# Top-k attention and an ELU layer: one chunk transposed later, weight differences one a step, two stores together

## The chip, the cores and the metric

The kernel runs on one core of a Trainium2 chip. A core has engines that run side by side, each through its own list of instructions in order: TensorE (PE; its weight loads are shown as PEld), VectorE (DVE), ScalarE (ACT), GpSimd (POOL) and SyncE (SP), which here only issues DMAs. They meet through semaphores. PE writes to PSUM, a small memory in banks of 512 float32 per partition; the other data lies in SBUF, 128 partitions wide. The metric is the device time of one execution in microseconds (us), the median of several runs.

## The reference

All is float32, apart from the layer's weights, which arrive as float64 and are taken apart by the kernel at the start.

```python
batch, n_heads, seq, head_dim = 8, 8, 576, 64
scores = q @ k.T / sqrt(64)                       # per head, 576 x 576
kth    = 32nd largest of each row
scores = where(scores >= kth, scores, -1e9)
attn   = softmax(scores)
x      = (attn @ v), heads joined                 # 4608 x 512
h      = x @ w_in                                 # 512 x 2048
g      = where(h > 0, h, exp(min(h, 0)) - 1)
out    = g @ w_out                                # 2048 x 512, out 4608 x 512
```

## The kernel before, in words

**Steps.** The attention is cut into 144 steps, 18 per batch element. A step is one tile of 128 queries for a pair of heads (in the last two steps of an element, or the first two, 64 queries of four heads). The main loop over `n` (L805) interleaves four stages of different tiles: scores of step n+2 on PE (`scores`, L326), the selection of the 32 largest of step n on DVE (`select`, L348: four MAX8 and three MATCH_REPLACE8 per head), the masked exponential of step n-1 on ACT and POOL (`spread` L373, `mask` L380, `normalise` L401), and of step n-2 the transposition of the probabilities on PE (`turn`, L418) with the product by v (`attend`, L443) when a group of tiles is complete.

**Turning.** The probabilities of a step are 2 x 576 columns, nine chunks of 128. `main` is chunks 0 to 3, `rest` is chunk 4 (the last keys of the first head and the first of the second), `other` is chunks 5 to 8. `main` and `other` go through PSUM tiles of a pool of two (`ps_t`), `rest` through columns 288 to 415 of a bank that also holds half of the scores of one head (`wide[1][:, 1, ...]`, columns 0 to 287). ACT copies each to SBUF (`et`, L434).

**The layer.** x is collected into blocks, 5 of one tile of 128 tokens at the start, 15 of two tiles, and one of one tile at the end. A block is a list of pieces: 16 `hidden` pieces (x @ w_in, ELU on ACT, POOL and DVE), and for a block of two tiles 7 `product` pieces (j = 0 to 6, and a last j = 7 that only empties a list), in which the product with w_out is made from seven products of half-size quarters, with sums on POOL (`combine`, L579). Four of the seven use differences of quarters of w_out (t1 to t4). These are made once on POOL, stored in DRAM (`kept`, L686) and streamed back for every block in tiles `tw` of two chunks from a pool of six (`stream`, L658; L666); a product consumes four such tiles and asks for a new one after each. `emit` (L582) stores one tile of a block's result.

**Order.** PE, ACT, DVE and POOL run in the order in which the program issues their instructions. SP is not in that list (L780): the order of its DMAs is set by the scheduler, which knows dependencies and its own estimates of time, and SP then works through that order without overtaking. `feed` (L763) is called four times a step, after each of DVE's four passes, and issues pieces of the layer when a running account says that they are due, so that the work is spread over the steps; what is left at the end follows in a row (L840). `at` (L741) puts loads and other calls at the start of a chosen step. In `load_halves` q and k of a head pair go into a pool of two buffers each (`kin`, `qin`), which DVE transposes into one of five `kqT` buffers (L289).

The step's own part of the loop, around the change:

```python
        if done:
            turn(done, main)
            turn(done, rest)
        if prev:
            mask(prev, 1, n <= tight)
        next(passes)
        feed(n, 0.25)
        if done:
            turn(done, other)
        next(passes)
        if prev:
            normalise(prev)
        feed(n, 0.25)
```

Of the kernel before, what the change touches and what calls it, by code (L numbers as in the profile page):

```python
# [9 lines left out]
ALU = mybir.AluOpType  # L10
FP32 = mybir.dt.float32
# [69 lines left out]
def kernel(  # L81
# [9 lines left out]
    nc = tc.nc  # L91
    P = nc.NUM_PARTITIONS
    B, H, S, D = q.shape
    dm, dff = moe_w_in.shape[0], moe_w_in.shape[1] // 2
# [9 lines left out]
    W = dm // 2  # L104
    TF, TB = 2, 6
    QT = NG // TF
# [294 lines left out]
    def normalise(u):  # L401

        if u.normal:
            return
        u.normal = True
        den = small.tile([P, 2], FP32, tag="dene", name="dene")
        nc.gpsimd.tensor_scalar_add(den[:], u.den[:, 0:2], EPS)  # L407
        rec = small.tile([P, 2], FP32, tag="rec", name="rec")
        nc.gpsimd.tensor_tensor(rec[:], den[:], power[:], ALU.pow)
        nc.gpsimd.tensor_tensor(den[:], den[:], rec[:], ALU.mult)  # L410
        nc.gpsimd.tensor_scalar(den[:], den[:], -1.0, 2.0, ALU.mult, ALU.add)
        nc.gpsimd.tensor_tensor(rec[:], rec[:], den[:], ALU.mult)
        for i in range(2):
            nc.gpsimd.tensor_scalar(  # L414
                u.sc[:, i, :], u.sc[:, i, :], rec[:, i : i + 1], 1.0, ALU.mult, ALU.mult
            )

    def turn(u, chunks):  # L418

        if u.turned:  # L420
            return
        g = u.group
        if g.et is None:
            g.et = etpool.tile([P, 2 * J + 1, len(g.tiles), P], FP32, tag="et", name="et")
        if chunks.stop - chunks.start == 1:
            ps = wide[1][:, 1, HS : HS + P]
        else:
            ps = ps_t.tile([P, JP], FP32, tag="t", name="eps")
        sc = u.sc[:, :, :].rearrange("p i s -> p (i s)")
        n = chunks.stop - chunks.start  # L430
        for c in range(n):
            c0 = (chunks.start + c) * P
            nc.tensor.transpose(ps[:, c * P : (c + 1) * P], sc[:, c0 : c0 + P], ident[:])  # L433
        nc.scalar.copy(  # L434
            g.et[:, chunks, u.at, :],
            ps[:, 0 : n * P].rearrange("p (c q) -> p c q", c=n),
        )
        if chunks.stop == 2 * J + 1:
            u.turned = True
            if u.at == len(g.tiles) - 1:  # L440
                closing.append(g)
# [68 lines left out]
    def ffn_pieces(blk):  # L510
# [71 lines left out]
        def emit(s):  # L582
            for t in blk.tiles[s]:
                p0 = t.cols.start - s * P
                nc.sync.dma_start(out[t.rows, :], blk.o[s][p0 : p0 + t.ql, :])

        def product(j):
            left, right = slice(0, W), slice(W, dm)
            while blk.after:
                blk.after.pop(0)()  # L590
            if j == 7:
                return
            if j == 0:
                close_gates(upto=(blk.number, NF - 1))
                blk.o = [opool.tile([P, dm], FP32, tag="osb", name="osb") for _ in range(2)]
                blk.e = [late["e"].tile([P, W], FP32, tag="e", name="e") for _ in range(2)]
                blk.s = [ps_f.tile([P, dm], FP32, tag="f", name="ops") for _ in range(2)]
            a11, a12 = quarter(0, 0), quarter(0, 1)
            a21, a22 = quarter(1, 0), quarter(1, 1)
            c11, c12 = blk.o[0][:, left], blk.o[0][:, right]  # L600
            c21, c22 = blk.o[1][:, left], blk.o[1][:, right]
            e0, e1 = blk.e[0][:], blk.e[1][:]
            one, two, three = blk.s[0][:, left], blk.s[1][:, left], blk.s[1][:, right]
            x, name, sums, opens, dst, after = (
                (a11, "b11", one, True, c11, [(a21, a21, a22, ALU.add)]),
                (a12, "b21", two, True, e0, [(a11, a21, a11, ALU.subtract)]),
                (a21, "t1", three, True, c22, [
                    (a12, a12, a11, ALU.subtract), (c11, c11, e0, ALU.add),
                ]),
                (a11, "t2", one, False, c12, [(a21, a22, a11, ALU.subtract)]),  # L610
                (a12, "b22", three, False, e1, [(c12, c12, e1, ALU.add)]),
                (a21, "t3", one, False, c21, [(c22, c22, c21, ALU.add)]),
                (a22, "t4", two, True, e0, [(c21, c21, e0, ALU.add)]),
            )[j]
            if j == 0:
                combine(*after.pop(0))
            for f in range(NG):
                if name[0] == "b":
                    w = w_out[:, NG * (name[1] == "2") + f, right if name[2] == "2" else left]
                else:  # L620
                    if f % TF == 0:
                        t = streamed.pop(0)
                    w = t[:, f % TF, :]
                nc.tensor.matmul(  # L624
                    sums, x[:, f, :], w, start=opens and f == 0, stop=f == NG - 1,
                    skip_group_check=not opens,
                )
                if name[0] == "t" and f % TF == TF - 1:
                    stream()
            if 0 < j < 4:  # L630
                combine(*after.pop(0))
            nc.scalar.copy(dst, sums)
            blk.after += [lambda x=x: combine(*x) for x in after]
            if j in (4, 6):
                blk.after.append(lambda: emit(j // 2 - 2))

        part = HIDDEN[blk.slots]
        behind = 2 * NF if blk.number else 0
# [27 lines left out]
        nc.sync.dma_start(t[:], src[:].rearrange("p (f n) -> p f n", f=TF))  # L666
        streamed.append(t)

    kept = {}

    def differences(q):

        fs = slice(q * TF, (q + 1) * TF)
        low = slice(NG + q * TF, NG + (q + 1) * TF)
        b11, b12 = w_out[:, fs, 0:W], w_out[:, fs, W:dm]
        b21, b22 = w_out[:, low, 0:W], w_out[:, low, W:dm]
        made = {}
        for name, x, y in (
            ("t1", b12, b11), ("t2", b22, "t1"), ("t4", b21, "t2"), ("t3", b22, b12),
        ):  # L680
            t = late["t"].tile([P, TF, W], FP32, tag="t", name="tw")
            made[name] = t
            y = made[y][:] if isinstance(y, str) else y
            nc.gpsimd.tensor_tensor(t[:], x, y, ALU.subtract)  # L684
            kept[name, q] = scratch.tile([P, TF * W], FP32, tag=f"{name}{q}", name="kept")
            nc.sync.dma_start(  # L686
                kept[name, q][:].rearrange("p (f n) -> p f n", f=TF), t[:]
            )

    ffn = []  # L690
    steps, first, due = [], {}, []
# [49 lines left out]
    def at(step, fn, *args):  # L741
        todo.setdefault(step, []).append((fn, args))
# [10 lines left out]
            at(f - ready, start_qk, b, hp)  # L753
            at(f - late_v, load_v, b, hp)

    for x in range(QT):
        at(first[1] - 2 + 2 * x, differences, x)
    for _ in range(TB):
        at(first[1] - 2 + 2 * QT, stream)

    fed = {"at": 0.0, "sum": 0.0, "over": 0.0}

    def feed(n, share):  # L763

        place[0] += 1
        close_gates(2 if n > tight + 3 else 6)
        fed["at"] = max(fed["at"], n)
        ahead = [(w - fed["sum"]) / (x - fed["at"]) for x, w in due if x > fed["at"]]
        if ahead:
            fed["over"] += max(0.0, share * min(ahead))  # L770
        fed["at"] += share
        while ffn and decoded[0] >= ffn[0][1] and 0.5 * ffn[0][0] <= fed["over"]:
            cost, _, piece, _ = ffn.pop(0)
            fed["over"] -= cost
            fed["sum"] += cost
            piece()
            settle()
# [27 lines left out]
    for n in range(NS + 3):  # L805
        for fn, args in todo.pop(n, []):
            fn(*args)
        ahead, cur, prev, done = step(n + 2), step(n), step(n - 1), step(n - 2)
        passes = select(cur, n < tight) if cur else iter(range(4))
        if prev and n > tight:  # L810
            spread(prev)
        next(passes)
        feed(n, 0.25)
        if ahead and n > 1:
            scores(ahead)
        while closing:
            attend(closing.pop(0))
        if prev:
            mask(prev, 0, n <= tight)
        if n > 1:  # L820
            turn_qk()
        next(passes)
        feed(n, 0.25)
        if done:
            turn(done, main)
            turn(done, rest)
        if prev:
            mask(prev, 1, n <= tight)
        next(passes)
        feed(n, 0.25)  # L830
        if done:
            turn(done, other)
        next(passes)
        if prev:
            normalise(prev)
        feed(n, 0.25)
        turn_qk(True)
        if n < 2:
            scores(ahead)
# [36 lines left out]
```

## Time and profile before

| what | us |
|---|---|
| median of 3 runs (lowest, highest) | 1604.12 (1603.91, 1605.75) |
| the profiled execution: its time, its span | 1605.63, 1603.8 |
| PE busy | 1523.6 (95%) |
| DVE busy | 1452.6 (91%) |
| ACT busy | 1200.0 (75%) |
| POOL busy | 903.3 (56%) |
| DMA queue of SP, share of 16 engines | 28.0% |

A line of the groups or of the timeline gives the kernel's line (L433), the engine, the operation, what it writes and reads by the program's names, and behind the bar or in brackets how long the engine was idle just before and what ended that. A line of the waits gives who waited for what, the total in us, how often, and the longest. PEld is PE's loading of weights, SPq is SP's queue of issues. A busy PE is modelled, since matmuls are pipelined; the granted clock is the share of full speed that TensorE had.

### The profile page before, as it was taken

To read this page: it belongs to the slowest core of one execution; us is meant where nothing else is said; L and a number is where in the kernel's file an instruction comes from. 1 tells how busy PE (TensorE), PEld (TensorE's weight loads), DVE (VectorE), ACT (ScalarE), POOL (GpSimd) and SP (SyncE) were. 2 spreads that over 40 slices of the span, in tenths; PEclk is the share of its full clock that TensorE was granted. 3 is DMA by queue.
4 is the path that set the end of the run, shared out by engine and by line. 5 is a ranking of instruction groups with operands and counts; after the bars stand their busy time and mean duration, and the time that the engine had idled before them with its cause. 6 is when DMAs were issued, how large, how long until landed. Compare 5 with 4: busy or idle time off the path is not lost.

```text
span 1603.8 us, 28233 instructions
## 1 busy us (share of the span) xinstructions
PE 1523.6 (95%) x9492; PEld 1182.3 (74%) x9492; DVE 1452.6 (91%) x2976; ACT 1200.0 (75%) x2460; POOL 903.3 (56%) x1551
## 2 busy tenths in 40 slices
PE   4789999999999999999999999998999999999999
PEld 2477667757777778876887788776777777877786
DVE  6999999999999799999999599999999969999700
ACT  6997676778686869695878787876878777878652
POOL 4984455446456465646565656564656565656550
PEclk9889989999999999999999999999999999999999
DMA  8622323012503251403421343114230413030411
GB/s 242 195 80 37 68 66 114 8 22 46 148 1 119 36 141 32 119 16 90 96 81 47 88 91 95 56 53 103 60 112 15 119 38 112 10 118 1 119 53 34
DMA packets 224912, 123.47 MB, mean 77 GB/s; under 512 B 182272, under 2 KB 183296, under 8 KB 224768
## 3 DMA queue, kind: packets, MB, share of 16 engines
q1 hardware_dynamic: 223568, 121.38, 28.0%
q8 instruction: 75, 1.23, 0.3%
q14 instruction: 69, 0.57, 0.1%
q10 hardware_dynamic: 1200, 0.30, 0.1%
HBM read 108.00 MB, written 13.63 MB: 76 GB/s over the span
## 4 chain that ended last, share of the span: by engine, by line
PE 67%; DVE 13%; ACT 11%; POOL 5%; issue 3%; DMA 1%; SPq 0%; DVEq 0%; ACTq 0%; POOLq 0%
PE hps L534 24%; PE ops L624 18%; PE avps L459 8%; PE scps L335 7%; DVE wk L362 6%; PE eps L433 5%; DVE m L369 4%; PE ops L562 2%; ACT sc L397 2%; ACT sc L343 2%; DVE m L355 2%; ACT sc L396 1%; POOL tw L684 1%; ACT et L434 1%; POOL sc L414 1%
## 5 line engine op out<-in xcount | busy, mean ns | idle before, releaser
L369 DVE MAX8 m<-wk 128x8 f32<-128x576 f32 x864 | 609.9, 747 | 3.3 <-POOL den L376 3.2
L534 PE MATMUL hps<-xT,w_in 128*128 128x256 f32 (+1 forms) x2688 | 550.8, 354 | 3.5 <-ACT gT L547 3.5
L534 PEld LDWEIGHTS hps<-xT,w_in 128*128 128x128 f32 x2688 | 442.9, 193 | 63.8 <-issue 15.5
L362 DVE MATCH_REPLACE8 wk<-m,wk 128x576 f32<-128x576 f32 x576 | 423.5, 743 | 0.0
L407 POOL TENSOR_SCALAR dene<-den 128x2 f32<-128x2 f32 x144 | 32.5, 226 | 471.7 <-ACT sc L397 470.4
L397 ACT ACTIVATE sc<-sc,den 128x576 f32<-128x576 f32 x288 | 223.4, 776 | 65.8 <-POOL den L376 51.2
L624 PE MATMUL ops<-tw,gT 128*128 128x256 f32 x960 | 224.5, 387 | 12.8 <-DMA tw<-kept 11.9
L396 ACT ACTIVATE sc<-sc,m 128x576 f32<-128x576 f32 x288 | 225.3, 782 | 11.5 <-DVE m L369 11.5
L343 ACT ACTIVATE sc<-scps 128x576 f32<-128x576 f32 x288 | 170.7, 645 | 73.5 <-PE scps L335 73.4
L414 POOL TENSOR_SCALAR sc<-sc,rec 128x576 f32<-128x576 f32 x288 | 214.4, 756 | 14.9
L335 PE MATMUL scps<-kqT 64*128 64x288 f32 (+1 forms) x1280 | 196.6, 447 | 25.5 <-ACT kqT L311 13.4
L355 DVE MAX8 m<-sc 128x8 f32<-128x576 f32 x288 | 202.2, 744 | 19.1 <-ACT sc L343 18.0
L624 PEld LDWEIGHTS ops<-tw,gT 128*128 128x128 f32 x960 | 178.9, 192 | 46.0 <-DMA tw<-kept 14.5
L362 DVE MATCH_REPLACE8 wk<-m,sc 128x576 f32<-128x576 f32 x288 | 211.7, 743 | 0.0
L459 PE MATMUL avps<-et,vT 128*64 128x256 f32 (+2 forms) x2320 | 197.0, 313 | 9.8 <-ACT et L434 9.8
L459 PEld LDWEIGHTS avps<-et,vT 128*64 128x64 f32 x2320 | 132.9, 142 | 82.2 <-issue 39.9
L504 POOL TENSOR_TENSOR gT<-n,gT 128x512 f32<-128x512 f32 x136 | 173.2, 1279 | 23.9 <-ACT n L553 23.9
L433 PE MATMUL eps<-ident,sc 128*128 128x128 f32 x1152 | 177.3, 279 | 0.5 <-POOL sc L414 0.4
L335 PEld LDWEIGHTS scps<-kqT 64*128 64x128 f32 (+1 forms) x1280 | 104.7, 183 | 94.4 <-issue 40.7
L434 ACT COPY et<-eps 128x512 f32<-128x512 f32 x288 | 164.6, 572 | 10.8 <-PE eps L433 8.4
L433 PEld LDWEIGHTS eps<-ident,sc 128*128 128x128 f32 x1152 | 142.4, 144 | 35.8 <-issue 13.3
L624 PE MATMUL ops<-w_out,gT 128*128 128x256 f32 x720 | 164.3, 381 | 0.1
(56 smaller groups left out, 1540.0 us busy)
## 6 DMA issues: line engine op xcount, KB each, us to landing
tw<-kept SPq DMA_DIRECT2D x240, 256.0 KB, 3.1
raw<-in_moe_w_in_dram SPq DMA_DIRECT2D x16, 512.0 KB, 4.9
vT<-in_v_dram SPq DMA_DIRECT2D x64, 128.0 KB, 2.5
raw<-in_moe_w_out_dram SPq DMA_DIRECT2D x16, 512.0 KB, 4.5
out_dram<-osb SPq DMA_DIRECT2D x32, 256.0 KB, 2.4
kin<-in_k_dram SPq DMA_DIRECT2D x112, 72.0 KB, 2.4
qin<-in_q_dram SPq DMA_DIRECT2D x112, 72.0 KB, 2.6
kept<-tw SPq DMA_DIRECT2D x16, 256.0 KB, 2.0
```

What stands on the lines that cost most here:

```text
L335: nc.tensor.matmul(wide[i][rows, half, 0:HS], kq[part, q0 : q0 + u.t.ql], kq[part, k0 : k0 + HS], start=True, stop=True,)
L343: nc.scalar.activation(u.sc[:, i, :].rearrange("p (a s) -> p a s", a=2), wide[i][:, :, 0:HS], AF.Copy, scale=scale,)
L355: nc.vector.max(found[i], cur[i])
L362: nc.vector.match_replace(wk[i], found[i], cur[i], TAKEN)
L369: nc.vector.max(found[i], cur[i])
L396: nc.scalar.activation(sc, sc, AF.Prelu, scale=-1.0, bias=low, alpha=1.0 / STEEP)
L397: nc.scalar.activation(sc, sc, AF.Exp, scale=-STEEP, bias=gap, accum_out=u.den[:, i : i + 1])
L414: nc.gpsimd.tensor_scalar(u.sc[:, i, :], u.sc[:, i, :], rec[:, i : i + 1], 1.0, ALU.mult, ALU.mult)
L433: nc.tensor.transpose(ps[:, c * P : (c + 1) * P], sc[:, c0 : c0 + P], ident[:])
L459: nc.tensor.matmul(ps[i * D : (i + 1) * D, cols], vt[:, 2 * J + i if c == J else i * J + c, :], w, start=(c == 0), stop=(c == J),)
L534: nc.tensor.matmul(blk.h[:, f % bank, :], w_in[:, i, f * P : (f + 1) * P], blk.xT[:, i, 0:n_tok], start=(i == 0), stop=(i == NC - 1),)
L624: nc.tensor.matmul(sums, x[:, f, :], w, start=opens and f == 0, stop=f == NG - 1, skip_group_check=not opens,)
```

## The change

It has three parts. (1) `turn(done, rest)` moves from directly behind `turn(done, main)` to directly ahead of `turn(done, other)`, so behind `mask(prev, 1)`, DVE's third pass and one call of `feed`. (2) The 16 subtractions that make t1 to t4 (four quarters of each) were issued four at a time at the start of steps 16, 18, 20 and 22; now one is issued in each of steps 16 to 31, behind `normalise` and ahead of the step's last `feed`, and its store with it. The first six streams move from the start of step 24 to the start of step 32. (3) The two stores of a block of two tiles, until now issued behind the sums of product 4 and of product 6, are both issued behind the sums of product 6. SP's order is left to the scheduler before and after.

```diff
             blk.after += [lambda x=x: combine(*x) for x in after]
-            if j in (4, 6):
-                blk.after.append(lambda: emit(j // 2 - 2))
+            if j == 6:
+                blk.after += [lambda s=s: emit(s) for s in range(2)]
...
-    def differences(q):
+    def difference(q, name, x, y):
         fs = slice(q * TF, (q + 1) * TF)
         low = slice(NG + q * TF, NG + (q + 1) * TF)
-        b11, b12 = w_out[:, fs, 0:W], w_out[:, fs, W:dm]
-        b21, b22 = w_out[:, low, 0:W], w_out[:, low, W:dm]
-        made = {}
-        for name, x, y in (
-            ("t1", b12, b11), ("t2", b22, "t1"), ("t4", b21, "t2"), ("t3", b22, b12),
-        ):
-            t = late["t"].tile([P, TF, W], FP32, tag="t", name="tw")
-            made[name] = t
-            y = made[y][:] if isinstance(y, str) else y
-            nc.gpsimd.tensor_tensor(t[:], x, y, ALU.subtract)
-            kept[name, q] = scratch.tile([P, TF * W], FP32, tag=f"{name}{q}", name="kept")
-            nc.sync.dma_start(
-                kept[name, q][:].rearrange("p (f n) -> p f n", f=TF), t[:]
-            )
+        ends = {
+            "b11": w_out[:, fs, 0:W], "b12": w_out[:, fs, W:dm],
+            "b21": w_out[:, low, 0:W], "b22": w_out[:, low, W:dm],
+        }
+        t = late["t"].tile([P, TF, W], FP32, tag="t", name="tw")
+        x, y = (ends[z] if z in ends else made[z, q] for z in (x, y))
+        nc.gpsimd.tensor_tensor(t[:], x, y, ALU.subtract)
+        made[name, q] = t[:]
+        kept[name, q] = scratch.tile([P, TF * W], FP32, tag=f"{name}{q}", name="kept")
+        nc.sync.dma_start(kept[name, q][:].rearrange("p (f n) -> p f n", f=TF), t[:])
...
-    for x in range(QT):
-        at(first[1] - 2 + 2 * x, differences, x)
+    spare = [(q, *names) for q in range(QT) for names in (
+        ("t1", "b12", "b11"), ("t2", "b22", "t1"), ("t4", "b21", "t2"), ("t3", "b22", "b12"))]
     for _ in range(TB):
-        at(first[1] - 2 + 2 * QT, stream)
+        at(first[1] - 2 + len(spare), stream)
...
         if done:
             turn(done, main)
-            turn(done, rest)
         if prev:
             mask(prev, 1, n <= tight)
         next(passes)
         feed(n, 0.25)
         if done:
+            turn(done, rest)
             turn(done, other)
         next(passes)
         if prev:
             normalise(prev)
+        if spare and n >= first[1] - 2:
+            difference(*spare.pop(0))
         feed(n, 0.25)
```

More of the change, by code (lines that the diff above doesn't have):

```diff
@@ L667, in stream @@
         streamed.append(t)
-    kept = {}
-    def differences(q):
+    kept, made = {}, {}
+    def difference(q, name, x, y):
         fs = slice(q * TF, (q + 1) * TF)
         low = slice(NG + q * TF, NG + (q + 1) * TF)
-        b11, b12 = w_out[:, fs, 0:W], w_out[:, fs, W:dm]
-        b21, b22 = w_out[:, low, 0:W], w_out[:, low, W:dm]
-        made = {}
-        for name, x, y in (
-            ("t1", b12, b11), ("t2", b22, "t1"), ("t4", b21, "t2"), ("t3", b22, b12),
-        ):
-            t = late["t"].tile([P, TF, W], FP32, tag="t", name="tw")
-            made[name] = t
-            y = made[y][:] if isinstance(y, str) else y
-            nc.gpsimd.tensor_tensor(t[:], x, y, ALU.subtract)
-            kept[name, q] = scratch.tile([P, TF * W], FP32, tag=f"{name}{q}", name="kept")
-            nc.sync.dma_start(
-                kept[name, q][:].rearrange("p (f n) -> p f n", f=TF), t[:]
-            )
+        ends = {
[8 more added lines that the diff above has]
+        nc.sync.dma_start(kept[name, q][:].rearrange("p (f n) -> p f n", f=TF), t[:])
     ffn = []
@@ L754 @@
             at(f - late_v, load_v, b, hp)
-    for x in range(QT):
-        at(first[1] - 2 + 2 * x, differences, x)
+    spare = [
+        (q, *names)
+        for q in range(QT)
+        for names in (
+            ("t1", "b12", "b11"), ("t2", "b22", "t1"), ("t4", "b21", "t2"),
+            ("t3", "b22", "b12"),
+        )
+    ]
     for _ in range(TB):
-        at(first[1] - 2 + 2 * QT, stream)
+        at(first[1] - 2 + len(spare), stream)
     fed = {"at": 0.0, "sum": 0.0, "over": 0.0}
```

## The prediction

> **What bounds the kernel now.** I read the chain first, then the windows, each engine's waits, and the timelines around the waits that the change touches. The chain of work that ended last, by engine:
>
> ```profile
> PE 67%; DVE 13%; ACT 11%; POOL 5%; issue 3%; DMA 1%; SPq 0%; DVEq 0%; ACTq 0%; POOLq 0%
> ```
>
> Busy times by window (length, then PE, PEld, DVE, ACT, POOL, granted clock):
>
> ```profile
> 286.00:546.00 260.00, 252.94 (x1454) 191.10 (x1452) 249.03 (x512) 203.91 (x416) 136.80 (x253) 1.00 0.22 55
> 560.00:921.00 361.00, 353.75 (x2251) 282.16 (x2255) 344.84 (x709) 276.94 (x572) 212.51 (x364) 1.00 0.30 79
> 1512.00:1603.80 91.80, 88.07 (x505) 71.33 (x504) 3.23 (x5) 40.54 (x84) 31.57 (x39) 1.00 0.15 47
> ```
>
> PE and DVE are both nearly full, and the last 92 us are PE alone. Who gives way shows in what DVE waited for (total, times, longest):
>
> ```profile
> DVE gT L506 <- ACT n L549: 73.6, 4, 65.0
> DVE kqT L289 <- PE scps L335: 37.4, 3, 14.2
> ```
>
> A step is 9.64 us of DVE without a gap (10.96 with two transposes), and DVE stands only where a kqT buffer still belongs to a PE that has fallen behind: 11.53 us at step 50, 11.63 at 86, 14.20 at 122, then in the tail. So from about step 18 PE's clock is the kernel's: a us that PE gains shortens the next of these stops, and the end comes sooner by as much. The reader looks for PE's own idle time:
>
> ```profile
> PE scps L433 <- ACT sc L343: 12.2, 17, 0.8
> PE ops L624 <- DMA tw<-kept: 11.9, 5, 5.0
> PE scps L335 <- ACT et L434: 11.4, 6, 2.6
> PE avps L459 <- ACT et L434: 9.8, 16, 1.9
> PE hps L534 <- ACT gT L547: 3.5, 2, 2.8
> ```
>
> **The differences.** Today four subtracts stand in one piece on POOL at steps 16, 18, 20 and 22, ahead of the tiny subtract (den) that ACT's Exp needs. POOL, ACT and PE around step 18:
>
> ```profile
> 215.94 1.27 POOL L684 TENSOR_TENSOR tw<-w_out 128x512 f32<-128x512 f32 x1
> 217.29 2.64 POOL L684 TENSOR_TENSOR tw<-w_out,tw 128x512 f32<-128x512 f32 x2
> 219.88 1.28 POOL L684 TENSOR_TENSOR tw<-w_out 128x512 f32<-128x512 f32 x1
> 221.11 0.20 POOL L376 TENSOR_TENSOR den<-m,m 128x2 f32<-128x2 f32 x1
> ...
> 217.38 0.78 ACT L396 ACTIVATE sc<-sc,m 128x576 f32<-128x576 f32 x1 [1.35 <-DVE m L369]
> 221.34 0.78 ACT L397 ACTIVATE sc<-sc,den 128x576 f32<-128x576 f32 x1 [3.18 <-POOL den L376]
> ...
> 225.05 1.95 PE L335 MATMUL scps<-kqT 64*128 64x288 f32 x6 [2.26 <-ACT et L434]
> ```
>
> PE pays 2.83 (200.6 us), 2.26 (225.1), 0.55, 0.42 and 2.59 (270.0): 8.65 us. Each long stop is followed by a slow clock: windows 200:210, 220:230, 270:280 were granted 0.66, 0.83, 0.67, which is 3.4 + 1.7 + 3.3 = 8.4 us of PE time. So 17 us could come back, but DVE caps it: the line at 217.38 is the last time ACT waits for DVE, and afterwards the least lag of ACT's first mask behind the last MAX8 of its tile is 6.8 us, at step 29. PE can't gain more than about 7 by then. The added side: 16 subtracts x 1.27 = the same 20.4 us on POOL, one a step behind normalise. At the dens of steps 17, 19, 21 and 25 Exp starts 0.03 us after den, so one there can delay Exp by 1.28; at 26 to 31 den is 1.5 to 3.2 us early, which hides it. Bounds: 0 (POOL is idle 2.3 to 6.5 us a step) to 10 x 1.28 = 12.8 at steps 16 to 25; even that leaves 4 of the 17. Nearest are the dens of steps 46 and 53, 2.1 us late without a PE gap: I take 1. The stores (16, landing in 2.0 us) go one a step into SP's queue; behind them stand v loads that are needed some 9 us later and outs that nobody awaits, so 0, up to 2 if that cover goes. The six first streams start at step 32 rather than 24, some 355 us; the first matmul on tw is at 398.7 and landing takes 3.1, so 0.
>
> **The last chunk later.** The chunk's transpose writes the bank whose other columns ACT is still copying (L343). PE around step 43:
>
> ```profile
> 478.80 0.66 PE L433 MATMUL eps<-ident,sc 128*128 128x128 f32 x4
> 480.23 0.30 PE L433 MATMUL scps<-ident,sc 128*128 128x128 f32 x1 [0.78 <-ACT sc L343]
> 480.37 3.62 PE L624 MATMUL ops<-w_out,gT 128*128 128x256 f32 x16
> ```
>
> Behind the 3.62 us of FFN the wait is over. Of 16 such waits after step 20, 13 have FFN next: 28 (0.38), 29, 31, 35, 43, 51, 99, 107, 115, 123, 135, 139 (0.78 each) and 130 (0.51), 9.5 us; at 67, 83 and 141 nothing lies between, and they stay. The copy (0.27, L434) moves behind mask (1.75) and the FFN's ACT work; mask starts 0.27 sooner, ACT's sum is the same, and the second half's copy ends when it did. New is that the next scores wait in that bank for the later copy. At steps 41, 49, 65, 81, 97, 105, 113, 121 they would come 0.8 to 1.3 us too soon, but there PE already waits 0.43 for the second half's copy just behind, so the next product starts when it does now. Bounds 0 to 8 x 1.3 = 10; nearest those rows: 0.
>
> **Both stores together.** SP stood 67 us in all before L585 stores, waiting for POOL's sums; the first store now yields to the streams of the last two products. Only at step 54 did tw come late behind it (0.96). osb is next written after 16 hidden pieces (16 x 1.73 = 28 us) against 2.4 to land; the last pair's stores have the last block's 28 us of PE. Gain 0 to 1, I take 0.
>
> **What is late next: tw.** SP takes its queue in order, and a kin load in it waits for DVE's transpose, at DVE's time:
>
> ```profile
> 408.04 0.31 SPq L235 DMA_DIRECT2D kin<-in_k_dram  x1
> 408.45 1.87 SPq L666 DMA_DIRECT2D tw<-kept  x4
> ...
> 411.70 1.99 PE L624 MATMUL ops<-tw,gT 128*128 128x256 f32 x8 [2.91 <-DMA tw<-kept]
> ```
>
> The like happens at 760.8 (2.39) and 1094.1 (5.04). SP's order is drawn by the scheduler, which sees PE sooner too and may put these streams ahead. If it puts the first four ahead, the next four still follow kin at some 411.5 + 3.1 = 415, against 421.2 when PE took the third tile of that product before: PE keeps about 6 of the 9.3 (7 + 3 x 0.78 at steps 29 to 35). At steps 71 and 103 PE is held until DVE's transpose as before, so 0.78 each of steps 51 and 99 is lost there.
>
> **Sum.** To step 50: -6, and -0.78 at 43; to 122: -1.56 (107, 115); behind: -2.85 (123, 130, 135, 139); new POOL delay +1, second pause in step 38 with a slow clock +1.7 (half of 3.4). Total -8.5. The profiled execution, 1605.63 us (span 1603.8), goes to 1597.1; it lies 1.51 above the median, so the median goes to 1595.6.
>
> **The clock rule.** At 1094.1 the 8 matmuls behind a 5.04 us stop took 3.78 us, against 1.99 for the 8 behind 2.91. The Trainium skill, "TensorE: Matmul & The Clock Gate", Part 1 on the clock gate, says PE falls to half clock after an idle window of about 3.4 us and needs about 3.4 us of work to return. The trace agrees as to the half, but 2.39 us was enough at 760.8 (window 755:765 at 0.83). By that rule alone the stop in step 38 would cost its full 3.4, and the sum would be -6.8.
>
> **Rivals.** (B) The queue lets go: both groups of streams go ahead. To step 50 PE gets 7 + 2.3 + 2.9 + 0.8, capped by DVE's stop (11.5 + 0.8 at step 24): -12.3 - 4.4 + 1 = -15.7: 1588.4. For it: only one kin stands ahead of the four streams. Against: the second group came 5 us later. (C) The order stays: PE reaches step 37 9.3 us sooner and waits until 411.70 all the same; 12 us idle halves the clock for 6.8 us (as windows 200:210 and 270:280): +3.4 - 0.8 - 4.4 + 1 = -0.8: 1603.3. (D) Slower: scores held by the late copy, at the wide bank, behind mask and FFN on ACT. For it: the 8 places, and 12 more where the second half's copy ends within 0.4 us of the last scores. Against: the absorbed 0.43 and an ACT that is idle 1 to 4 us in most steps. 20 x 1.0 = 20: 1595.6 + 20 = 1615.6; it turns the sign from 9 such steps. The Trainium skill, "PSUM — Partial Sum Buffer", on bank collisions, tells to order accesses by bank, not address; the wait at 480.23 agrees. (E) The new queue order holds PE at two more products as at 1094.1 (5.04 + 3.4 each): 1595.6 + 16.9 = 1612.5; one alone gives no change.
>
> **Chances.** Forecast 0.36, B 0.23, C 0.19, D 0.09, E 0.13. Within 0.2% (3.2 us, about what a measurement can tell from none) lie C and a little of E and the forecast: 0.20. Faster: forecast and B, 0.59. Slower: 0.21. The range, 1586 to 1610, takes in all but half of D and E and the lowest of B; the faster cases alone span 1586 to 1600.
>
> **What would show it.** No L684 block before den and no Exp wait over 2 us at steps 16 to 24, the clock 1.0 there; the L433 wait down from 12.2 to about 3; DVE's first stop shorter than 11.5 by PE's gain; tw waits at steps 37 to 39, 71 and 103 tell B from C; L335 waits for et beyond step 30 mean D. Wrong if SP holds tw elsewhere.

## The result: 0.3% slower

The changed kernel takes 1610.1 us (median of 7 runs, 1608.72 to 1610.78) against 1605.0 (1602.26 to 1606.41) of the kernel before beside it: 1.0033 of the time [1.0021, 1.0044], 5.1 us more. The profiled execution took 1609.76 us, its span 1607.6, which is 3.8 more than the span before. One of the six runs of the change with SP in order, further below, was slow (1752.97 us at a granted clock of 0.851), and the time given there is the median of the other five.

**Profile after.** The chain of work that ended last, by engine, runs through DVE for 29% of the span (13% before) and through PE for 55% (67% before). Where PE stands, the chain goes on in what PE waited for:

```profile
PE 55%; DVE 29%; ACT 9%; issue 4%; POOL 1%; DMA 1%; SPq 0%; DVEq 0%; ACTq 0%; POOLq 0%
```

Busy times by window, columns as in the prediction (length, then PE, PEld, DVE, ACT, POOL, granted clock):

```profile
286.00:546.00 260.00, 247.06 (x1407) 189.15 (x1407) 247.48 (x509) 196.72 (x400) 143.20 (x252) 0.98 0.26 69
560.00:921.00 361.00, 353.26 (x2225) 281.40 (x2224) 347.15 (x714) 273.56 (x564) 212.31 (x362) 0.99 0.29 77
```

In the first window PE and DVE both lost: PE is busy 5.9 us less than before, DVE 1.6 us, and the clock is no longer full. What PE waited for (total, times, longest):

```profile
PE scps L335 <- ACT et L434: 36.7, 24, 5.2
PE ops L624 <- DMA tw<-kept: 17.5, 5, 10.6
...
PE scps L433 <- ACT sc L343: 2.3, 3, 0.8
```

The wait of the chunk's transpose fell from 12.2 to 2.3, as expected. But the scores' wait for `et` rose from 11.4 to 36.7. The product by v waited 9.8 for the same copies before; that wait is gone from the list, so waiting for `et` grew by 36.7 - 21.2 = 15.5. Of this growth 9.1 us lie in the first 114 us, where DVE is busy for 62.4 of the 64 us from 50 to 114 and loses 0.3 us by it (its lead over the kernel before goes from 1.3 to 1.0); only 6.4 come later, where PE sets the pace. The wait for `tw` grew by 5.6, with one stop of 10.6. And DVE, which waits where a kqT buffer still belongs to a late PE, waited 6.0 us more than before (43.4 against 37.4):

```profile
DVE kqT L289 <- PE scps L335: 43.4, 3, 16.1
```

Its stops at steps 50, 86 and 122 are 15.45, 11.80 and 16.09 us, against 11.53, 11.63 and 14.20. DVE is 1.8 us ahead of the kernel before up to step 50, 2.1 behind after it, 4.6 after step 86 and 6.7 after step 122. PE's tail behind DVE's last step then is 2.9 shorter: 3.8. (DVE's waits for ACT's copies of the scores, 20.2 us against 18.0, are in these numbers too.)

**Where the differences' gain went.** The subtracts no longer hold ACT. POOL and ACT at step 18, the place shown in the prediction:

```profile
214.47 1.28 POOL L681 TENSOR_TENSOR tw<-w_out,tw 128x512 f32<-128x512 f32 x1
...
217.21 0.20 POOL L376 TENSOR_TENSOR den<-m,m 128x2 f32<-128x2 f32 x1 [1.05 <-DVE m L369]
```

```profile
216.44 0.78 ACT L396 ACTIVATE sc<-sc,m 128x576 f32<-128x576 f32 x1 [1.42 <-DVE m L369]
217.44 0.78 ACT L397 ACTIVATE sc<-sc,den 128x576 f32<-128x576 f32 x1 [0.23 <-POOL den L376]
```

One subtract stands ahead of den, and is done before DVE's maxima are: Exp waits 0.23 us instead of 3.18. Over the kernel this wait of ACT fell from 51.2 to 36.7. PE's first transposes of step 36 start at 396.26, where they started at 405.86 before: 9.6 us ahead. PE before, then PE of the changed kernel from step 36 on, and SP's queue in the same stretch:

```profile
405.86 0.66 PE L433 MATMUL eps<-ident,sc 128*128 128x128 f32 x4
```

```profile
396.26 0.66 PE L433 MATMUL eps<-ident,sc 128*128 128x128 f32 x4
...
397.30 1.89 PE L624 MATMUL ops<-tw,gT 128*128 128x256 f32 x8
409.81 3.67 PE L624 MATMUL ops<-tw,gT 128*128 128x256 f32 x8 [10.63 <-DMA tw<-kept]
413.42 0.76 PE L335 MATMUL scps<-kqT 64*128 64x288 f32 x4
```

```profile
406.21 0.31 SPq L235 DMA_DIRECT2D kin<-in_k_dram  x1
406.62 1.87 SPq L666 DMA_DIRECT2D tw<-kept  x4
```

SP's order at this place is the old one: one kin load, then four streams. The kin load waits for DVE's transpose, which comes when DVE's own pace brings it, 1.8 us sooner than before. So the streams start 1.83 us sooner (406.62 against 408.45) although PE is 9.6 sooner, and PE stands for 10.63 us instead of 2.91. The stop also slowed the clock. Windows of after around it:

```profile
400.00:410.00 10.00, 0.19 (x1) 0.19 (x2) 10.00 (x21) 1.07 (x4) 6.15 (x10) 0.65 0.25 66
410.00:420.00 10.00, 10.00 (x46) 7.85 (x47) 10.00 (x23) 4.68 (x9) 0.00 (x0) 0.84 0.89 219
```

The clock was at half for 10.24 us, most of them idle, and the 8 matmuls behind the stop took 3.67 us instead of 1.99. PE's scores after it start at 413.42, against 413.62 before: 9.4 of the 9.6 us are gone within one step.

**Where the loss came from.** The step 42, in which the copy of the last keys' chunk is late. PE after, ACT after, and PE before:

```profile
461.01 1.89 PE L534 MATMUL hps<-xT,w_in 128*128 128x256 f32 x8
462.83 0.75 PE L335 MATMUL scps<-kqT 64*128 64x288 f32 x2
464.83 1.23 PE L335 MATMUL scps<-kqT 64*128 64x288 f32 x6 [1.25 <-ACT et L434]
466.00 2.38 PE L459 MATMUL avps<-et,vT 128*64 128x256 f32 x20
```

```profile
464.00 0.63 ACT L553 ACTIVATE n<-n 128x512 f32<-128x512 f32 x1
464.53 0.25 ACT L434 COPY et<-scps 128x128 f32<-128x128 f32 x1
464.68 0.59 ACT L434 COPY et<-eps 128x512 f32<-128x512 f32 x1
```

```profile
463.26 1.24 PE L335 MATMUL scps<-kqT 64*128 64x288 f32 x8
464.43 0.65 PE L459 MATMUL avps<-et,vT 128*64 128x256 f32 x2
465.50 2.37 PE L459 MATMUL avps<-et,vT 128*64 128x256 f32 x18 [0.42 <-ACT et L434]
```

Before, PE issued all eight scores and two matmuls of the product, and then waited 0.42 for the copy of the second half. Now two scores go, and six wait 1.25 us for the small copy at 464.53, which stands on ACT behind the mask and the ELU of the layer. When it is done PE still has 1.23 us of scores ahead of the product, so the second half's copy is not what it waits for any more: the old wait of 0.42 is replaced by one of 1.25, not joined with it. Stops of 1.25 to 1.30 us like this are at 464.8, 547.7, 712.1, 884.1, 1048.9, 1137.4, 1220.3 and 1303.1, at 0.6 to 0.7 us net each. At steps 58, 74 and 90 the same hold costs another 0.7 each without showing as a stop: the eight scores take 2.1 to 2.2 us there, 1.24 before. At steps 50 and 122 DVE's stop ends with these very scores; they end 3.2 us after their start, 1.2 before, which puts DVE 2.0 us later at both.

By the starts of PE's scores, the changed kernel is 0.2 us ahead of the one before at step 38 and 5.1 behind at step 128. The eleven holds are 7.4 us, and a slow clock behind that of step 66 is 1.7 (see the last section). Against them stand 3.4 us from two waits for `tw`, that of step 54, which is gone, and the one at 1094, which is 3.66 us instead of 5.04 with less slow clock behind it.

The waits that the chunk's move did save came back as longer scores. At step 43, PE after, ACT after, and PE before:

```profile
479.79 3.62 PE L624 MATMUL ops<-w_out,gT 128*128 128x256 f32 x16
483.24 0.27 PE L433 MATMUL scps<-ident,sc 128*128 128x128 f32 x1
...
483.88 2.09 PE L335 MATMUL scps<-kqT 64*128 64x288 f32 x8
```

```profile
484.42 0.27 ACT L434 COPY et<-scps 128x128 f32<-128x128 f32 x1
```

```profile
484.35 1.24 PE L335 MATMUL scps<-kqT 64*128 64x288 f32 x8
```

The wait of 0.78 ahead of the chunk's transpose is gone, but the eight scores take 2.09 where they took 1.24: 0.85 more. It is the same hold: the third of the eight starts at 484.74, when ACT's small copy is done (484.42 + 0.27), after a pause too short to be listed as a wait of its own. So it went at 8 of the 13 places whose wait was saved.

### The profile page after: what moved, and what is told of

The parts are those of the page before. It is cut to its first block, busy times and chain, and to the rows that moved or that the text cites. A ratio compares the mean times of both kernels' runs of the same rounds, so it can differ in the third digit from the quotient of the medians.

```text
span 1607.6 us, 28204 instructions
## 1 busy us (share of the span) xinstructions
PE 1520.4 (95%) x9492; PEld 1184.1 (74%) x9492; DVE 1451.4 (90%) x2976; ACT 1200.3 (75%) x2460; POOL 904.2 (56%) x1551
## 3 DMA queue, kind: packets, MB, share of 16 engines
q8 instruction: 75, 1.23, 0.3%
## 4 chain that ended last, share of the span: by engine, by line
PE 55%; DVE 29%; ACT 9%; issue 4%; POOL 1%; DMA 1%; SPq 0%; DVEq 0%; ACTq 0%; POOLq 0%
PE hps L534 19%; PE ops L624 17%; DVE wk L362 13%; DVE m L369 10%; PE avps L459 7%; PE scps L335 7%; PE eps L433 4%; DVE m L355 4%; ACT sc L397 2%; ACT sc L396 2%; ACT sc L343 1%; DMA tw<-kept 1%; DVE raw L192 1%; ACT n L553 1%; ACT et L434 1%
## 5 line engine op out<-in xcount | busy, mean ns | idle before, releaser
L335 PE MATMUL scps<-kqT 64*128 64x288 f32 (+1 forms) x1280 | 214.9, 445 | 50.7 <-ACT et L434 36.7
L397 ACT ACTIVATE sc<-sc,den 128x576 f32<-128x576 f32 x288 | 223.4, 776 | 51.7 <-POOL den L376 36.7
L355 DVE MAX8 m<-sc 128x8 f32<-128x576 f32 x288 | 202.4, 745 | 20.2 <-ACT sc L343 20.2
L335 PEld LDWEIGHTS scps<-kqT 64*128 64x128 f32 (+1 forms) x1280 | 113.6, 182 | 130.1 <-ACT et L434 51.8
L459 PE MATMUL avps<-et,vT 128*64 128x256 f32 (+2 forms) x2320 | 186.5, 311 | 0.0
L459 PEld LDWEIGHTS avps<-et,vT 128*64 128x64 f32 x2320 | 127.4, 141 | 66.9 <-issue 27.2
```

The source lines that it names most:

```text
L335: nc.tensor.matmul(wide[i][rows, half, 0:HS], kq[part, q0 : q0 + u.t.ql], kq[part, k0 : k0 + HS], start=True, stop=True,)
L355: nc.vector.max(found[i], cur[i])
L397: nc.scalar.activation(sc, sc, AF.Exp, scale=-STEEP, bias=gap, accum_out=u.den[:, i : i + 1])
L459: nc.tensor.matmul(ps[i * D : (i + 1) * D, cols], vt[:, 2 * J + i if c == J else i * J + c, :], w, start=(c == 0), stop=(c == J),)
```

## The experiments

The theory after the result had two parts: the chunk's late copy holds the scores (the prediction's D), and SP's order holds tw (its C), so that what the differences gain is lost at step 37. The rivals were that the differences themselves brought less than they seemed to, that the stores disturbed SP's queue, and that the loss lay in the interplay of parts rather than in the chunk.

**The parts alone.** The four runs here share one set of runs of the kernel before (1604.40 us).

Only the chunk's transpose moved:

```diff
             turn(done, main)
-            turn(done, rest)
...
         if done:
+            turn(done, rest)
             turn(done, other)
```

> Only the last keys' chunk is turned later; the differences stay four at a time and the stores apart. Theory H (the hold): ACT's late copy of the chunk keeps the bank, and the scores of the next step, not only their last two products but all six that touch either bank of that tile, wait for it: about 0.7 us of PE net at steps 42, 50, 58, 66, 74, 82, 90, 98, 106, 114 and 122; those before a tw wait that is there anyway (71, 103) are absorbed in it, the rest is not: +4.5 us, waits of scores for et up to 25 us or more in total, waits of the chunk for ACT's copy of the scores down to 2 or 3 us. Theory Q (SP's order alone makes the change slower): no change or up to 5 us faster, as predicted for this part.

1614.44 us, 1.0071 [1.0057, 1.0084]: 10 us slower, twice what was expected. PE's waits of this run:

```profile
PE scps L335 <- ACT et L434: 46.7, 23, 5.4
```

Waiting for `et` rose by 25.5 over the kernel before (21.2); 11.6 of this lies in the first 114 us, where DVE loses 0.5 us by it. Alone the move also pays where the differences still stand in a block, since the small copy now is behind the Exp that waits for den. PE and ACT at step 18:

```profile
220.57 0.75 PE L335 MATMUL scps<-kqT 64*128 64x288 f32 x2
225.98 2.29 PE L335 MATMUL scps<-kqT 64*128 64x288 f32 x6 [4.66 <-ACT et L434]
```

```profile
220.72 0.78 ACT L397 ACTIVATE sc<-sc,den 128x576 f32<-128x576 f32 x1 [2.91 <-POOL den L376]
...
225.69 0.24 ACT L434 COPY et<-scps 128x128 f32<-128x128 f32 x1
```

The stop there is 4.66 us, 2.26 before. So the chunk's move is a loss by itself, and no interplay is needed to make it one.

Only the differences, one a step (the part of the change's diff from `differences` to `difference`, the `spare` list and the later first streams):

```diff
+        if spare and n >= first[1] - 2:
+            difference(*spare.pop(0))
```

> Only the differences are spread, one a step. Theory Q: PE is 6 to 8 us ahead by step 36 and loses all of it at step 37, where tw still stands behind a kin load that waits for DVE; the wait there grows from 2.9 to about 10 us and PE's clock halves for 7 to 10 us behind it: between -1 and +3 us in all. If the differences themselves cost (POOL late for den in 16 steps), PE is not ahead at step 36 and the time is 3 to 5 us longer. If the gain is carried (the prediction), 6 to 7 us shorter.

1606.06 us, 1.0012 [1.0003, 1.0021]. PE was 8.1 us ahead at steps 24 to 35 and 0.4 behind at step 38. The tw wait there is 9.60, with the clock at half for 10.24 us. The gain was made, and was lost at the same place, as theory Q expected.

Only the stores:

```diff
-            if j in (4, 6):
-                blk.after.append(lambda: emit(j // 2 - 2))
+            if j == 6:
+                blk.after += [lambda s=s: emit(s) for s in range(2)]
```

> Only the two stores of a pair go out together. All theories: between -1.5 and +0.5 us; the tw wait at step 54 (0.96 us) gone. If the stores' place has a part in the slowdown, over +1 us with longer tw waits.

1604.86 us, 1.0007 [0.9998, 1.0016]: no difference. The tw wait at step 54 is gone, as the diff would have it, and the four that remain sum to 10.2 (11.9 before).

Differences and stores, without the chunk:

> The change without the chunk's move. Theory H: without the holds the slowdown is gone, between -3 and +1 us against before, so some 5 us faster than the changed kernel; waits of scores for et back to about 10 us. Theory Q alone: as slow as the changed kernel, +4 to +5 us.

1605.41 us, 1.0009 [1.0000, 1.0018]. The whole change costs 1610.1, so the chunk's move costs 4.7 us on top of these two as well. Both of them do nothing for the time under this order of SP.

**SP in the program's order.** If SP's order is what eats the gain, an order in which the streams are not behind the kin loads returns it. The scheduler is told to keep SP's instructions as the program issues them:

```diff
-    engines = {E.PE, E.Activation, E.DVE, E.Pool}
+    engines = {E.PE, E.Activation, E.DVE, E.Pool, E.SP}
```

With the kernel before otherwise:

> The kernel before with SP's DMAs in the order in which the program issues them, so that no stream of tw stands behind a kin load of a later batch. Theory Q: the tw waits of before (2.9 + 1.0 + 0.6 + 2.4 + 5.0 = 11.9 us) go to under 2 us and the half clock behind those of steps 71 and 103 (1.7 + 3.4 us) with them: 12 to 17 us shorter. Rival (the streams are held by something else, or new waits in program order replace these): within 3 us of before, or longer.

1629.82 us against 1605.64, 1.0154 [1.0140, 1.0168]: the theory expected a gain and the rival, new waits in the program's order, held. PE's waits in this run, and one block's place in it, SP and then PE:

```profile
PE ops L624 <- DMA tw<-kept: 28.1, 15, 6.2
```

```profile
492.06 4.76 SPq L666 DMA_DIRECT2D tw<-kept  x5
509.21 0.34 SPq L585 DMA_DIRECT2D out_dram<-osb  x1
509.64 5.49 SPq L666 DMA_DIRECT2D tw<-kept  x8
```

```profile
512.43 2.35 PE L624 MATMUL ops<-tw,gT 128*128 128x256 f32 x8 [1.29 <-DMA tw<-kept]
```

The first store of a block stands ahead of eight streams, and waits for POOL's sum of that tile (the piece of 0.73 us at 508.45 on POOL, `osb<-osb,e`). From 496.8 to 509.21 SP issues nothing. So in the program's order the store takes the place that kin had, in 14 of the 15 blocks: 15 waits instead of 5.

That store is the very thing that the third part of the change moves. With differences and stores, SP in order and the chunk where it was:

> Differences one a step and stores together, the chunk where it was, and SP's DMAs in program order. Theory Q: PE's 8 to 10 us of step 36 is no longer taken away at step 37; DVE's stop at step 50 falls from 11.5 us to under 3; with the tw waits gone 20 to 26 us shorter than before, and 8 to 10 shorter than before with SP in program order. Rival (the gain of the differences is lost whatever SP does): as long as before with SP in program order.

1580.74 us, 0.9850 [0.9837, 0.9864]: 24.9 us faster than before, and 49.1 faster than before with SP in order, where 8 to 10 were expected: the store's place had not been counted. No wait for tw is listed. PE at step 37:

```profile
398.70 3.62 PE L624 MATMUL ops<-tw,gT 128*128 128x256 f32 x16
402.25 1.24 PE L335 MATMUL scps<-kqT 64*128 64x288 f32 x8
```

Sixteen matmuls in one piece, where there were eight, a stop and eight. SP itself waits for DVE's transposes much less (first row, before; second, this run):

```profile
SPq L235 <- DVE kqT L289: 359.9, 22, 49.9
```

```profile
SPq L235 <- DVE kqT L289: 67.7, 8, 17.4
```

PE's sum of it, against before: tw -11.9, `et` -4.7, hps -1.3, busy time -10.1 (1513.5 against 1523.6, at a mean granted clock of 0.992 against 0.982), the chunk's wait +0.6: -27.4, of which the span shows -25.1. DVE's three stops are 2.38, 9.51 and 10.51.

**What each part is worth with SP in order.** Three more kernels complete the table (before: 1604.19 beside them).

The whole change with SP in order:

> The changed kernel, whole, with SP's DMAs in program order. Theories H and Q together: 4 to 9 us longer than differences and stores with SP in program order (1580.7), from the holds of the moved chunk, so 1585 to 1590, and some 20 us shorter than the changed kernel. If the holds matter only beside the queue's waits: 1580.

1590.44 us, 0.9918 [0.9905, 0.9931]. No wait for tw; waiting for `et` is 39.2 us instead of 16.5 (6.0 of the scores and 10.5 of the product), 12.1 of the growth in the first 114 us, and the chunk's wait is 2.3 instead of 12.8. The time is 9.7 us longer than 1580.74, a little more than the 4 to 9 expected: the chunk's move costs as much as it did alone. The same eleven holds are in this trace, and at two of them, those of steps 50 and 122, the clock fell to half for 3.41 us behind the stop of 1.29.

Stores only, SP in order:

> The kernel before with the stores together and SP in program order; the differences stay four at a time. If the first store's wait for POOL in front of the streams is what made SP's program order slow (1629.8), its tw waits (28 us) are gone and the time is 1587 to 1592: the tw waits of before saved, but not the 8 to 10 us of the differences. Rival (the early stream or the differences' stores did it): still over 1610.

1591.27 us, 0.9915 [0.9903, 0.9927]. Differences only, SP in order:

> Differences one a step, SP in program order, the first store where it was, behind product 4. The first store then stands before the streams of products 5 and 6 and waits for POOL's sum in most of the 15 blocks: tw waits of 20 us or more, 1610 to 1625. Rival (the stores' place is nothing, as predicted): 1580, as with the stores together.

1620.45 us, 1.0101 [1.0086, 1.0115], with 27.7 us of waits for tw.

| kernel | SP by the scheduler | SP in order |
|---|---|---|
| before | 1604.2 to 1605.6 | 1629.8 |
| chunk only | 1614.4 | not run |
| differences | 1606.1 | 1620.5 |
| stores | 1604.9 | 1591.3 |
| differences and stores | 1605.4 | 1580.7 |
| all three (the change) | 1610.1 | 1590.4 |

Read by columns: the differences gain nothing in the first (they stand 0.5 to 1.7 us higher), 9 to 11 us in the second. The stores are worth nothing in the first and 38 to 40 in the second. The chunk costs 5 to 10 in the first and 10 in the second.

**What is it that the scores wait for?** The chunk shares a bank with half 1 of the second head's scores. If the wait were for the bank, the half 0 of that head, in another bank of the same tile `wide[1]`, could go. In the stop shown above two of eight scores went, and those are half 0 of the first head; so half 0 of the second head waited already. A test is to issue the scores head by head:

```diff
-        for half in range(2):
-            for h, i, rows in u.heads:
+        for h, i, rows in u.heads:
+            for half in range(2):
```

> The changed kernel with the score products of a head one behind the other (both halves of the keys), not the two heads in turn, so that the tile with the chunk's bank is written by the last four records. Theory H with order kept by whole tile: the scores run 4 records and wait before the other 4; each hold leaves 0.6 us of work behind the copy rather than 0.9, so 0.3 us less at 11 places and 3 us in all at most. If order is kept by the bank alone, the wait now falls before the last 2 records. If the holds do not make the slowdown: no change.

The first head's four go, and the second head's four wait. PE of this kernel at step 42:

```profile
463.43 1.24 PE L335 MATMUL scps<-kqT 64*128 64x288 f32 x4
465.43 1.23 PE L335 MATMUL scps<-kqT 64*128 64x288 f32 x4 [0.76 <-ACT et L434]
```

By a wait for the bank it would have been six and two. So the wait is for the whole tile. The stop is 0.76 instead of 1.25, and waiting for `et` 27.1 instead of 36.7. The time is 1609.13, 1.0027 [1.0016, 1.0038]: 1.0 less than the change, which the intervals do not tell from none.

The same on the best kernel (differences, stores, SP in order):

> As the run with differences, stores and SP's program order, with the scores by head as well: ACT can copy the first head while PE writes the second, so the chunk's wait for that copy (0.78 us, 12 us in all) falls to about 0.2. Theory: 3 to 8 us shorter than without the scores by head. Rival (ACT's copies wait elsewhere): the same.

1580.05 us, 0.9847 [0.9834, 0.9861], against 1580.74: no difference, and the chunk's wait stays at 11.9 (12.8). This was a miss: the gain on PE's own row that was hoped for did not appear, since the waits of the chunk's transpose are for ACT's copy of the scores, which their order on PE hardly moved.

## Why the prediction was wrong

The forecast was 1595.6 with a range of 1586 to 1610; the time was 1610.1, just outside, with a sign that got 0.21. The chances of C (0.19) and of D (0.09) were set as if one excluded the other; both came true, C by its mechanism and D at eleven places with some 0.7 us each, not at 20 with 1.0. By terms: the differences with the stores were forecast at -6 + 1 + 1.7 = -3.3 and measured +1.0 (1605.41 against 1604.40); the chunk was forecast at -5.2 and measured +4.7. So the chunk's term is the larger of the two failures.

**Right: PE sets the pace, and DVE's stops carry it on.** DVE's stops grew and shrank with PE in every run, down to 2.38 us at step 50 with differences and stores and SP in order.

**Right: the differences bring PE forward, up to DVE's cap.** Worked out: 7 for the differences, and 2.3 for three saved waits of the chunk, 9.3 us by step 37. Measured: 9.6 (8.1 with the differences alone). The cap is right: against DVE, which itself was 1.8 us sooner (1.3 with the differences alone), PE gained 7.2 and 6.8. The closeness of 9.3 and 9.6 is luck. PE was 9.0 ahead at step 24 already, so the chunk's three waits gave 0.6, not 2.3; and about 1.0 of DVE's 1.8 comes from the start, where the first key load was awaited 1.09 us less. The added subtract behind normalise delayed nothing that shows at step 18 (the sum had 1 for it).

**Wrong in size and in choice: the tw queue, "if it puts the first four ahead ... PE keeps about 6 of the 9.3".** The scheduler did not put them ahead: one kin load and four streams stood there in the same order after as before. The sum took a reordering that nothing in the profile showed for certain, where the order of before was at hand as the nearest row; that row gave rival C. C's idle time was close: 12 us were worked out, 10.63 were measured. Behind the stop PE was 0.2 us ahead of the kernel before, since the streams came 1.83 us sooner and the slow clock took 1.68 back.

**Its clock.** The forecast took 1.7 us of slow clock here, C 3.4. The eight matmuls behind the stop lost 1.68 (3.67 against 1.99): the forecast's size was right. The clock was at half from 403.0 to 413.2, that is, from 3.8 us after PE's last matmul (397.30 + 1.89) to 3.4 us after work resumed at 409.81. Only the last 3.4 us had work in them, and half of that is the 1.7 lost. The Trainium skill, "TensorE: Matmul & The Clock Gate", Part 1 on the clock gate, gives about 3.4 us for the idle window and for the return, and the trace agrees at this stop; the prediction read the loss by that rule as the full 3.4, where work at half clock for 3.4 us loses 1.7.

**Wrong: the chunk's hold, "but there PE already waits 0.43 for the second half's copy just behind, so the next product starts when it does now".** This is the term that set the sign. The prediction named the eight steps and a hold of 0.8 to 1.3 us, bounded the whole by 0 to 10 us, and took 0. The step left out what lies between the two waits. The wait that the hold was to be absorbed in stands behind the scores and the product's first two matmuls; the hold stands ahead of six of the eight scores. They are 1.23 us of work that used to run during the second half's copy and now run after it, so 0.6 to 0.7 us remain of each. That it is six and not fewer follows from the wait for the whole tile, shown by the head-by-head order. And the 9.5 us that the 13 saved waits were to bring came back in the main: at step 43 as 0.85 us within the scores. The chunk's part was to give a gain of up to 9.5, of which the sum kept 0.78 + 1.56 + 2.85 = 5.2; it cost 10.0 alone and 4.7 on top of the other two parts. The profiles show where the two differ. Alone, PE is 3.5 us later than before at step 36, since the chunk's copy then stands behind the Exp that waits for the differences' block (the stop of 4.66 us at step 18 is one of these), and still 1.3 later at step 39. On top of the other two it is level at step 36 and 1.2 ahead at step 39. From step 39 to step 141 the chunk takes 6.3 and 5.7 us, nearly the same.

**Right, but by luck of SP's order: the stores at 0.** Under the scheduler's order the step is right as worked out (the wait at step 54 went). In the program's order the first store is the worst instruction in SP's queue. The prediction's "SP stood 67 us in all before L585 stores" was the hint that it didn't follow up.

**Rival E** (tw later at two more products) did not occur: tw waits at 760 and 1094 are 1.79 and 1.06, and 3.66, against 2.39 and 5.04. Rival B, the queue letting go (1588.4), is what the runs with SP in order did: without the chunk's move 1580.7, with it 1590.4.

**What stays open.** Why the scheduler left the kin load ahead of the streams wasn't tried. Nor was the chunk's move alone with SP in order. Nor was a chunk in a tile of its own, which would take the hold away and keep its move. In the run with SP in order alone, 16.2 of the 24 us are more waiting for tw (28.1 against 11.9) and 9.5 a longer busy time of PE. Behind its later stops the clock is at half for 17.1 us from step 50 on, against 10.2 before, which can explain some 3.4 of the 9.5; the rest was not traced.

## What to carry to other kernels

When an engine is made faster, ask of every queue that feeds it what the feed itself waits for: here a stream that was ready stood behind a load tied to another engine's pace, and the gain of 9.6 us ended there in one step. A wait is only absorbed by a later one if no work of the same engine lies between the two; count the instructions between them. And two parts that each measure as nothing may be worth 1.5% together with a third, so parts of a change are worth trying in pairs, and the part that harms (here the chunk) on its own.

## What the runs showed of the hardware that was not expected

**Short stops can slow the clock too.** Behind the stop of 1.25 us at 712.1 the clock was at half for 3.41 us; the product there took 4.07 us for what took 2.38 behind the same stop at 464.8. PE there, and the window around it (granted clock 0.72):

```profile
712.10 1.23 PE L335 MATMUL scps<-kqT 64*128 64x288 f32 x6 [1.25 <-ACT et L434]
713.26 4.07 PE L459 MATMUL avps<-et,vT 128*64 128x256 f32 x20
```

```profile
712.00:718.00 6.00, 5.90 (x29) 3.41 (x30) 6.00 (x12) 2.35 (x6) 2.67 (x4) 0.72 0.00 0
```

In the kernel with the scores head by head the same followed three stops of 0.76, 0.76 and 0.80 us (at 712.8, 1047.1 and 1299.9; the product took 4.02 to 4.07 us). Yet the seven other stops of 1.25 to 1.30 us of the changed kernel were followed by a full clock, and so was the stop of 2.91 us before, at 411.7 (1.00 from 410 to 420). So the length of one stop does not decide; what does was not settled. By the idle window of about 3.4 us alone that the Trainium skill, "TensorE: Matmul & The Clock Gate", Part 1 on the clock gate, gives, 1.25 us would cost nothing; the measurement differs.

**The order of one queue is worth more than any of the three parts under the scheduler's order.** With the same work on every engine, the kernel before took 1605 or 1630 us by the order of SP's queue alone, and with that order fixed by the program the place of one store a block made it 1630 or 1591.
